# Hash attention and routed experts on one core: order of the small transfers at the start, queue of one small input, cut of the output stores

## The chip, the core and the metric

The kernel runs on one core of a Trainium2 chip. The metric is the device time of one execution in microseconds (us), and lower is better. The kernel before took 804.9 us (median of three runs, 802.9 to 805.1). Engines are named as the profile names them: PE is TensorE (matmuls), DVE is VectorE, ACT is ScalarE, POOL is GpSimd, SP is the sync engine. SPq, ACTq and POOLq are their queues of DMA issues. The core's 16 DMA engines serve all of these queues.

A profile is one execution under the hardware profiler. Its times count from the start of the span, and its span is about 1.7 us shorter than the timed execution (804.0 against 805.68 us for the kernel before).

## The reference, cut to what matters

```python
# q, k, v: (4, 8, 768, 64) float32; proj: (64, 6)
q_bits = (einsum('bhsd,dk->bhsk', q, proj) > 0)      # six hash bits for each row
k_bits = (einsum('bhsd,dk->bhsk', k, proj) > 0)
mask = bucket(q_bits)[..., :, None] == bucket(k_bits)[..., None, :]
attn = softmax(where(mask, q @ k.T / 8, -1e9));  x = attn @ v        # -> (3072, 512)
P = sinkhorn(exp(x @ w_gate - max))                  # eight rounds, 8 experts
out = sum over e of P[:, e] * (relu(x @ w1[e]) @ w2[e])              # (3072, 512)
```

## The kernel before

Attention goes first, in eight head groups of four heads each. The PE work of a group is 24 units of scores, exp and values. For a group's scores the kernel needs q and k transposed with the head dimension on partitions, and their hash bits beneath them in the same tile. DVE transposes 32x32 blocks, POOL casts to float16, and small DMAs ("stackings", 48 KB each) move the blocks of each head to partitions 0 to 63. The bits are computed by float32 matmuls with `pb`, which is built from `proj`, written to DRAM in one transfer ("put") and read back per head ("bit transfers"). This is the head of the kernel and one group's preparation:

```python
for c in range(2):
    pin(nc.sync.dma_start(out=proj4[:, c, :], in_=proj[32*c:32*(c+1), :].unsqueeze(0)
                          .to_broadcast([HG, 32, NB])))          # HG = 4
nc.vector.memset(pb, 0.0)
for a in range(HG):                                              # DVE copies of proj
    nc.vector.tensor_copy(pb[32*a:32*(a+1), :, a, 0:NB], proj4[32*a:32*(a+1)])
# ...
def stack(name, c):
    for h in range(HG):
        pin(eng(name).dma_start(out=d[name][32*c:32*(c+1), h, :],
                                in_=t16s[name][32*h:32*(h+1), c, :]))
def get_bits(name):
    for h in range(HG):
        pin(eng(name).dma_start(out=d[name][D:KR, h, :]..., in_=dss[name][:, h, 0:NB+1, :]...))
# ... prepare(n), in pieces between the units of group n - 1 (group 0: all at once)
turn_qk("k", 0);  stack("k", 0);  turn_qk("k", 1)
if n: stack("k", 1);  fetch(n + 1, "k")                          # fetch: POOL's queue
turn_qk("q", 0);  turn_qk("q", 1)
hashed("k");  put_bits("k")
if n == 0: stack("k", 1);  get_bits("k")
stack("q", 0);  hashed("q");  put_bits("q");  stack("q", 1)
if n: fetch(n + 1, "q");  get_bits("k")
get_bits("q");  cast_v();  fetch(n + 1, "v" if n else "kqv")
```

`pin` keeps the order of the program on each queue.

The experts come after that. In the last expert each block of 128 output rows is stored as it is ready. Row r*24 + j*4 + m of a batch lies on partition m*32 + r, so the output side of a store has the dimensions (m: 4, r: 32, columns: 512):

```python
outv = out.rearrange("(b r j m) d -> b j m r d", b=B, r=R, j=J)
# in the fused blocks (batches 0 to 2 of the last expert), two stores of 256 KB each:
pin(nc.sync.dma_start(out=outv[b, j], in_=sums_of(b, j).rearrange("p c d -> p (c d)")))
# in final() (the last batch), six blocks, the last in two halves of the columns:
pin((nc.sync if cols.start == 0 else nc.scalar).dma_start(out=outv[b, j][:, :, cols], in_=dst[:, cols]))
```

The softmax here doesn't subtract the row's maximum and nothing guards it: scores larger than these inputs give would overflow.

Of the kernel before, what the change touches and what calls it, by code (L numbers as in the profile page):

```python
# [20 lines left out]
def kernel(  # L21
# [11 lines left out]
    nc = tc.nc  # L33
    B, H, S, D = q.shape
    assert (B, H, S, D) == (4, 8, 768, 64)
    NB = proj.shape[1]
# [4 lines left out]
    DD = H * D  # L41
# [9 lines left out]
    HG = 4  # L51
    NGRP = H // HG
    R = 32
    M = S // R
    KT = S // P
    M4 = P // R
    QT = S // HG
    KR = D + NB + 1
# [4 lines left out]
    def pin(ins):  # L63
        tc.keep_in_program_order(ins)
        return ins
# [2 lines left out]
    pb = consts.tile([P, 2, HG, 8], F32)  # L68
    proj4 = consts.tile([P, 2, NB], F32)
    for c in range(2):  # L70
        pin(nc.sync.dma_start(out=proj4[:, c, :], in_=proj[32 * c:32 * (c + 1), :].unsqueeze(0)
                              .to_broadcast([HG, 32, NB])))
    nc.vector.memset(pb, 0.0)
    for a in range(HG):
# [50 lines left out]
    outv = out.rearrange("(b r j m) d -> b j m r d", b=B, r=R, j=J)  # L125

    def sums_of(b, j):
        if j < J // 2:
            return acc[:, b, j, 0:2, :]
        return acc[:, b, j - J // 2, 2:4, :]  # L130

    def quarters_of_w(e):

# [94 lines left out]
    def mixed(e, b):  # L228

        wq = weights[e, "t"]  # L230
        pw = pw_[-1]
        for i in range(J // 2):
            hq = hsums[e, b, i]
            plo, phi = pw[:, b * J + i, e:e + 1], pw[:, b * J + J // 2 + i, e:e + 1]
            if e == 1:
                for j in (i, J // 2 + i):
                    pin(nc.scalar.activation(out=sums_of(b, j), in_=sums_of(b, j), func=Act.Copy,
                                             scale=pw[:, b * J + j, 0:1]))
            a = yps.tile([P, DD // 2], F32, tag="y", name="a")
            d1 = yps.tile([P, DD // 2], F32, tag="y", name="d1")  # L240
            y2 = y2ps.tile([P, DD // 2], F32, tag="y", name="y2")
            vt = vkeep.tile([P, 4, DD // 2], F32, tag="v", name="vt")

            def prod(dst, hn, wn, first):
                for fo in range(FH):
                    pin(nc.tensor.matmul(dst, hq[hn][:, fo, :], wq[wn][:, fo, :], start=first and fo == 0,  # L246
                                         stop=fo == FH - 1, skip_group_check=True))

            def keep(k, p):
                pin(nc.scalar.activation(out=vt[:, k], in_=a, func=Act.Copy, scale=p))  # L250

            def gather(k, src, p):
                dst = acc[:, b, i, k, :]
                pin(nc.vector.scalar_tensor_tensor(out=dst, in0=src, scalar=p, in1=dst, op0=Alu.mult, op1=Alu.add))  # L254

            def step(name):
                if name == "a1":
                    prod(a, "h11", "b11", True)
                    keep(0, plo)
                elif name == "a2":  # L260
                    prod(a, "s2", "t2", False)
                    keep(2, phi)
                elif name == "a3":
                    prod(a, "s1", "t1", False)
                    keep(3, phi)
                elif name == "a4":
                    prod(a, "s4", "b22", False)
                    keep(1, plo)
                elif name == "d":
                    prod(d1, "h12", "b21", True)  # L270
                    gather(0, d1, plo)
                elif name == "y":
                    prod(y2, "s3", "t3", True)
                    gather(3, y2, phi)
                else:
                    prod(y2, "h22", "t4", False)
                    gather(2, y2, phi)

            for g, name in enumerate(ORDERS[i]):
                step(name)  # L280
                if g == 4 and i + 1 < J // 2:
                    sums_of_h(e, b, i + 1)
                if g == 6:
                    if e < E - 1:
                        pin(nc.gpsimd.dma_start(out=acc[:, b, i], in_=vt, accum_op=Alu.add))  # L285
                    else:
                        eng = nc.vector if i == J // 2 - 1 else nc.gpsimd
                        pin(eng.tensor_tensor(acc[:, b, i], acc[:, b, i], vt, op=Alu.add))
                        for j in (i, J // 2 + i):
                            pin(nc.sync.dma_start(out=outv[b, j],  # L290
                                                  in_=sums_of(b, j).rearrange("p c d -> p (c d)")))
                    next(coming)
                yield 433

    def final():

        e, b = E - 1, B - 1
        w2, hT = weights[e, 2], hts[e, b]
        for j in range(J):
            yp = (yps if j % 3 < 2 else y2ps).tile([P, DD], F32, tag="y", name="yp")  # L300
            dst = sums_of(b, j).rearrange("p c d -> p (c d)")
            for cols in ((slice(0, DD),) if j < J - 1 else (slice(0, DD // 2), slice(DD // 2, DD))):
                for fo in range(FO):
                    pin(nc.tensor.matmul(yp[:, cols], hT[:, fo, j * P:(j + 1) * P], w2[:, fo, cols],
                                         start=(fo == 0), stop=(fo == FO - 1), skip_group_check=True))
                pin(nc.vector.scalar_tensor_tensor(out=dst[:, cols], in0=yp[:, cols],
                                                   scalar=pw_[-1][:, b * J + j, e:e + 1], in1=dst[:, cols],
                                                   op0=Alu.mult, op1=Alu.add))
                pin((nc.sync if cols.start == 0 else nc.scalar).dma_start(out=outv[b, j][:, :, cols],
                                                                          in_=dst[:, cols]))  # L310
            yield

    def first_hidden(b):
# [49 lines left out]
    def prepare(n):  # L363

        d = grp[n] = {}
        va, vs = vas[n % 2], vss[n % 2]
        trs, bts, dss, t16s = {}, {}, {}, {}
# [2 lines left out]
            d[name] = wk.tile([P, HG, S], F16, tag=name + "s", name=name + "s")  # L370
            t16s[name] = wk.tile([P, 2, S], F16, tag="t16", name="t16")

        def eng(name):
            return nc.scalar if n == 0 and name == "q" else nc.sync

        def turn_qk(name, c):
            i_ap = nat[name, n][:, :, 32 * c:32 * (c + 1)]
            o_ap = trs[name][:, c, :]
            if name == "k":
                i_ap = i_ap.rearrange("p (m t) d -> p m t d", m=M4)  # L380
                o_ap = o_ap.rearrange("p (t m r) -> p m t r", t=KT, m=M4)
            else:
                o_ap = o_ap.rearrange("p (m r) -> p m r", r=R)
            pin(nc.vector.transpose(o_ap, i_ap))  # L384
            pin(nc.gpsimd.tensor_copy(t16s[name][:, c, :], trs[name][:, c, :]))  # L385

        def stack(name, c):
            for h in range(HG):
                pin(eng(name).dma_start(out=d[name][32 * c:32 * (c + 1), h, :],  # L389
                                        in_=t16s[name][32 * h:32 * (h + 1), c, :]))  # L390

        def hashed(name):
            pr = ops.tile([P, 512], F32, tag="o", name="pr")
# [14 lines left out]
            pin(eng(name).dma_start(out=ds.rearrange("j h r t -> (j h r) t"), in_=bts[name]))  # L408
            dss[name] = ds

        def get_bits(name):
            for h in range(HG):
                pin(eng(name).dma_start(out=d[name][D:KR, h, :].rearrange("r (j t) -> r j t", j=HG),
                                        in_=dss[name][:, h, 0:NB + 1, :].rearrange("j r t -> r j t")))

        def cast_v():
            v32 = wk.tile([P, HG, 3, D], F32, tag="v32", bufs=1)
# [10 lines left out]
        lag = 2 if n > 2 else 1  # L428
        yield 0
        turn_qk("k", 0)  # L430
        stack("k", 0)
        yield lag
        turn_qk("k", 1)
        if n:
            stack("k", 1)
            if n + 1 < len(groups):
                fetch(n + 1, "k")
        yield 2 * lag
        turn_qk("q", 0)
        yield 3 * lag  # L440
        turn_qk("q", 1)
        yield 2 + 3 * lag
        hashed("k")
        put_bits("k")
        if n == 0:
            stack("k", 1)
            get_bits("k")
        stack("q", 0)
        yield 4 + 3 * lag
        hashed("q")  # L450
        put_bits("q")
        stack("q", 1)
        if n and n + 1 < len(groups):
            fetch(n + 1, "q")
        yield 6 + 3 * lag
        if n:
            get_bits("k")
        get_bits("q")
        cast_v()
        if n + 1 < len(groups):  # L460
            fetch(n + 1, "v" if n else "kqv")
# [92 lines left out]
    for _ in prepare(0):  # L554
        pass
    warm = ops.tile([P, 512], F32, tag="o", name="warm")
    for _ in range(12):
        pin(nc.tensor.matmul(warm, ident, vas[1].rearrange("p h t d -> p (h t d)")[:, 0:512],
                             start=True, stop=True))

# [9 lines left out]
    for u in range(len(units) + 1):  # L570
        if u < len(units):
            n, h, kt = units[u]
            b, g = groups[n]
# [24 lines left out]
        elif u >= 2 * per:  # L598
            owed += (total if b < 3 else total - 12 * 865) / (2 * per - 8)
            while owed > 0:  # L600
                c = next(fill, None)
# [199 lines left out]
```

## Time and profile before

| what | before | view |
|---|---|---|
| span | 804.0 us | page |
| first score matmul | 21.07 us | timeline |
| first scores of group 1 | 48.24 us, after 6.07 us of idle PE | timeline |
| first scores of group 2 | 70.3 us | timeline |
| last DVE instruction ends | 787.7 us | timeline |

The page of the kernel before: span, PE's busy time, its busy tenths in 40 slices of 20 us, the granted clock in tenths, and the busy share of the DMA engines in tenths.

```profile
span 804.0 us, 16754 instructions
...
PE   3969999999999999999999999999999999999991
...
PEclk9779999999989999999999999999999999999996
DMA  6966676641002264486468657745964676541222
```

PE is busy 90% of the time or more except in the first and third slice and in the last one. The change aims at the time there. The timeline of the kernel before at the start (start, duration, engine, line, operation, output<-input, and in brackets the engine's idle time ahead of it and what ended it):

```profile
0.80 1.38 SPq L71 DMA_DIRECT2D proj<-in_proj_dram  x2
2.22 0.48 SPq L354 DMA_DIRECT2D acc<-in_k_dram  x1
...
4.05 0.98 DVE L76 COPY pb<-proj 32x12 f32<-32x12 f32 x4 [3.05 <-DMA proj<-in_proj_dram]
...
6.60 1.84 DVE L384 STREAM_TRANSPOSE acc<-acc 128x768 f32<-128x768 f32 x2 [0.82 <-DMA acc<-in_k_dram]
...
10.02 3.69 SPq L389 DMA_DIRECT2D ks<-t  x4
...
21.07 1.44 PE L473 MATMUL st<-qs,ks 71*128 71x384 f16 x4 [4.84 <-DMA qs<-ds]
...
48.24 0.80 PE L473 MATMUL st<-qs,ks 71*128 71x384 f16 x2 [6.07 <-DMA qs<-ds]
```

`proj` is 6 KB with its four copies, goes first in the sync queue and is there at 4.05 us. Both starts of scores wait for bits of q (`qs<-ds`). The windows view of the kernel before (stretch, length, then busy time and instructions of PE, PEld, DVE, ACT and POOL; then the granted clock, the busy share of the DMA engines, and GB/s):

```profile
50.00:52.00 2.00, 2.00 (x18) 1.22 (x16) 1.26 (x3) 1.41 (x2) 0.00 (x0) 0.50 0.00 0
5.00:8.00 3.00, 0.36 (x8) 0.20 (x8) 2.05 (x7) 0.00 (x0) 0.35 (x1) 1.00 0.99 400
788.00:790.00 2.00, 0.00 (x0) 0.00 (x0) 0.00 (x0) 0.00 (x0) 0.00 (x0) 0.99 0.26 102
```

The first line shows a clock of 0.50 after the idle gap. In the third, only stores run, on a quarter of the DMA engines' time at a quarter of the rate of the second. The timeline of the kernel before at its end, DVE's last instruction and the last store issues:

```profile
778.67 14.92 SPq L309 DMA_DIRECT2D out_dram<-acc  x6
...
787.24 0.48 DVE L306 SCALAR_TENSOR_TENSOR acc<-yp,p,acc 128x256 f32<-128x256 f32 x1 [1.13 <-PE yp L304]
```

Six issues take 14.92 us, and the span ends 16.3 us after the last computation.

### The profile page before, as it was taken

The page shows a single profiled execution, that of the slowest core. Times are in us where ns is not written, and L with a number is a line of the kernel's source. Part 1 is how long each engine was busy: PE and PEld are TensorE (multiplying, and loading weights), DVE is VectorE, ACT ScalarE, POOL GpSimd, SP SyncE. Part 2 cuts the span into 40 slices and gives each one's busy share as a digit, 9 for nine tenths or more (in the row PEclk, how much of TensorE's full clock was granted, in tenths as well). Part 3 has the DMA queues.
Part 4 walks back from the last instruction along what each step waited for, and adds up shares of the span by engine and source line. Part 5 has one row for each costly group of instructions (what it writes and reads, how often), then busy time and mean ns, then how long its engine had stood idle before and what let it go on. Part 6 is the DMA issues. An engine that isn't in the chain of part 4 may idle for free.

```text
span 804.0 us, 16754 instructions
## 1 busy us (share of the span) xinstructions
PE 756.1 (94%) x6384; PEld 523.1 (65%) x6384; DVE 531.0 (66%) x1198; ACT 509.1 (63%) x1022; POOL 310.1 (39%) x314
## 2 busy tenths in 40 slices
PE   3969999999999999999999999999999999999991
PEld 1546656656655677777777777777777777777750
DVE  3334555645458677777777777777777777778760
ACT  0758666767844677766666666666666666666530
POOL 7645356238300133344444334344434434242220
PEclk9779999999989999999999999999999999999996
DMA  6966676641002264486468657745964676541222
GB/s 169 268 161 150 145 196 159 140 113 51 2 2 52 42 111 84 81 156 106 93 112 139 115 96 133 122 94 96 162 106 83 121 139 106 95 89 62 84 80 92
DMA packets 42636, 88.56 MB, mean 110 GB/s; under 512 B 9852, under 2 KB 22908, under 8 KB 42556
## 3 DMA queue, kind: packets, MB, share of 16 engines
q0 software_dynamic: 27440, 71.06, 45.6%
q1 hardware_dynamic: 14316, 15.82, 7.0%
q8 instruction: 50, 0.82, 0.4%
q10 hardware_dynamic: 800, 0.62, 0.3%
q14 instruction: 30, 0.25, 0.1%
HBM read 53.14 MB, written 7.08 MB: 75 GB/s over the span
## 4 chain that ended last, share of the span: by engine, by line
PE 79%; DMA 6%; ACT 5%; DVE 2%; POOL 2%; SPq 2%; issue 2%; POOLq 0%; ACTq 0%; DVEq 0%
PE a L679 18%; PE a L246 17%; PE d L679 13%; PE y L246 8%; PE st L473 5%; PE d L246 4%; PE hp L531 4%; PE yp L206 3%; ACT pt L476 2%; PE num L489 2%; DMA qs<-t 2%; PE hp L321 2%; DMA qs<-ds 1%; PE yp L541 1%; SPq L389 1%
## 5 line engine op out<-in xcount | busy, mean ns | idle before, releaser
L688 DVE CUSTOM_DVE_ANT_0 hT<-d,u 128x384 f16<-128x384 f32 x336 | 185.6, 553 | 99.8 <-ACT u L684 98.1
L250 ACT ACTIVATE vt<-a,p 128x256 f32<-128x256 f32 x324 | 153.3, 473 | 149.2 <-PE a L246 148.9
L476 ACT ACTIVATE pt<-st 128x768 f16<-128x768 f32 x192 | 147.1, 809 | 71.7 <-PE st L473 51.3
L684 ACT COPY u<-a 128x384 f32<-128x384 f32 x336 | 160.9, 479 | 22.4 <-PE a L679 20.1
L285 POOL DMA_DIRECT2D acc<-vt x72 | 61.4, 852 | 267.9 <-ACT vt L250 112.3
L246 PEld LDWEIGHTS <-hT 128*128 128x128 f16 x1296 | 126.3, 97 | 50.7 <-DVE hT L688 1.1
L246 PE MATMUL a<-t,hs 128*128 128x256 f16 x972 | 145.8, 272 | 2.0 <-ACT vt L250 1.5
L246 PEld LDWEIGHTS <-hs 128*128 128x128 f16 x972 | 94.8, 98 | 38.3 <-issue 2.8
L473 PE MATMUL st<-qs,ks 71*128 71x384 f16 x384 | 98.0, 338 | 15.9 <-DMA qs<-ds 11.7
L679 PEld LDWEIGHTS <-t 128*128 128x128 f16 x896 | 87.7, 98 | 36.1
L679 PE MATMUL a<-xT,s 128*128 128x384 f16 x448 | 109.4, 326 | 0.1
L679 PE MATMUL d<-xd,t 128*128 128x384 f16 x448 | 109.4, 326 | 0.0
L246 PE MATMUL y<-t,hT 128*128 128x256 f16 x648 | 97.1, 272 | 0.0
L254 DVE SCALAR_TENSOR_TENSOR acc<-y,p,acc 128x256 f32<-128x256 f32 x162 | 77.4, 478 | 11.4 <-PE y L246 11.4
L489 PEld LDWEIGHTS <-pt 128*128 128x128 f16 x1152 | 62.5, 99 | 28.4 <-issue 3.7
L679 PEld LDWEIGHTS <-s 128*128 128x128 f16 x672 | 65.5, 97 | 17.6 <-issue 2.3
L489 PE MATMUL num<-va,pt 128*128 128x65 f16 x1152 | 68.4, 196 | 0.6 <-ACT pt L476 0.6
L385 POOL CAST t<-acc 128x768 f16<-128x768 f32 x32 | 26.3, 826 | 89.5 <-DVE acc L384 89.3
L473 PEld LDWEIGHTS <-ks 71*128 71x128 f16 x384 | 33.4, 100 | 37.1 <-issue 14.7
L718 ACT ACTIVATE hT<-a 128x384 f16<-128x384 f32 x112 | 54.0, 482 | 1.8 <-PE a L679 1.7
L679 PE MATMUL a<-xd,s 128*128 128x384 f16 x224 | 54.3, 323 | 0.7 <-ACT u L684 0.5
L679 PE MATMUL a<-xT,t 128*128 128x384 f16 x224 | 54.7, 326 | 0.0
(97 smaller groups left out, 981.2 us busy)
## 6 DMA issues: line engine op xcount, KB each, us to landing
acc<-vt POOLq DMA_DIRECT2D x72, 512.0 KB, 4.6
t<-in_moe_w_dram POOLq DMA_DIRECT2D x24, 512.0 KB, 7.5
out_dram<-acc SPq DMA_DIRECT2D x23, 256.0 KB
acc<-in_k_dram POOLq DMA_DIRECT2D x7, 768.0 KB, 5.6
acc<-in_q_dram POOLq DMA_DIRECT2D x7, 768.0 KB, 6.0
v<-in_v_dram POOLq DMA_DIRECT2D x28, 192.0 KB, 4.6
t<-in_moe_w_dram POOLq DMA_DIRECT2D x4, 1024.0 KB, 10.1
ks<-t SPq DMA_DIRECT2D x64, 48.0 KB
```

The source lines that it names most:

```text
L246: pin(nc.tensor.matmul(dst, hq[hn][:, fo, :], wq[wn][:, fo, :], start=first and fo == 0, stop=fo == FH - 1, skip_group_check=True))
L250: pin(nc.scalar.activation(out=vt[:, k], in_=a, func=Act.Copy, scale=p))
L254: pin(nc.vector.scalar_tensor_tensor(out=dst, in0=src, scalar=p, in1=dst, op0=Alu.mult, op1=Alu.add))
L285: pin(nc.gpsimd.dma_start(out=acc[:, b, i], in_=vt, accum_op=Alu.add))
L473: pin(nc.tensor.matmul(st[:, i, 0:HT], d["k"][0:KR, h, kt * P:(kt + 1) * P], d["q"][0:KR, h, i * HT:(i + 1) * HT], start=True, stop=True))
L476: pin(nc.scalar.activation(out=pt, in_=st[:, :, 0:HT], func=Act.Exp, scale=scale))
L489: pin(nc.tensor.matmul(num[:, j * (D + 1):(j + 1) * (D + 1)], pf[:, j * P:(j + 1) * P], va[:, h, kt, :], start=(kt == 0 and j == 0), stop= ...
L531: pin(nc.tensor.matmul(hp[:, 0:HT], w1[:, do, fo * P:(fo + 1) * P], xT[:, do, b * S + t * HT:b * S + (t + 1) * HT], start=(do == 0), stop= ...
L679: pin(nc.tensor.matmul(bk, wq[wn][:, do, f * P:(f + 1) * P], xq[xn][:, do, :], start=first and do == 0, stop=do == 1, skip_group_check=True))
L684: pin(nc.scalar.copy(t, bk))
L688: pin(add(TENSOR_ADD_SAT, out=dst, in0=bk, in1=u, s0=3e38, s1=0.0))
L718: pin(nc.scalar.activation(out=hT[:, f, hi], in_=a, func=Act.Relu))
```

## The change

It has three parts. Head-by-head order: each operand's first head is stacked and gets its bits first, so that scores can begin before the other heads are ready; in group 0, q's first two heads go on ACT's queue and the rest on SP's. `proj` moves to ACT's queue, so that the first large load is issued earlier. A store is cut into four transfers of 32 partitions.

```diff
-        pin(nc.sync.dma_start(out=proj4[:, c, :], in_=proj[32 * c:32 * (c + 1), :].unsqueeze(0)
+        pin(nc.scalar.dma_start(out=proj4[:, c, :], in_=proj[32 * c:32 * (c + 1), :].unsqueeze(0)
...
+    def put_rows(b, j, src, cols, engs):
+        for m in range(M4):
+            pin(engs[m % len(engs)].dma_start(out=outv[b, j][m][:, cols], in_=src[R * m:R * (m + 1), cols]))
...   (fused blocks: put_rows(..., (nc.sync,));  final(): put_rows(..., (nc.sync, nc.scalar)))
-            return nc.scalar if n == 0 and name == "q" else nc.sync
+            return nc.scalar if n == 0 and name == "q" and h < 2 else nc.sync
...
-        def stack(name, c):
-            for h in range(HG):
+        def stack(name, h):
+            for c in range(2):
...   (get_bits(name, h): one head, no loop)
         turn_qk("k", 1)
+        stack("k", 0)
         if n:
             stack("k", 1)
...
         turn_qk("q", 1)
+        stack("q", 0)
...      (both puts, stack("k", 1) for n == 0, stack("q", 1), stack("k", 2), fetch of q)
+        get_bits("k", 0);  get_bits("q", 0);  get_bits("k", 1);  get_bits("q", 1)
+        stack("k", 3);  stack("q", 2);  get_bits("k", 2);  get_bits("q", 2)
+        stack("q", 3);  get_bits("k", 3);  get_bits("q", 3)
         cast_v()
...
-    for _ in range(12):          # warm-up matmuls
+    for _ in range(14):
```

More of the change, by code (lines that the diff above doesn't have):

```diff
@@ L289, in mixed @@
                         for j in (i, J // 2 + i):
-                            pin(nc.sync.dma_start(out=outv[b, j],
-                                                  in_=sums_of(b, j).rearrange("p c d -> p (c d)")))
+                            put_rows(b, j, sums_of(b, j).rearrange("p c d -> p (c d)"), slice(0, DD), (nc.sync,))
                     next(coming)
@@ L308, in final @@
                                                    op0=Alu.mult, op1=Alu.add))
-                pin((nc.sync if cols.start == 0 else nc.scalar).dma_start(out=outv[b, j][:, :, cols],
-                                                                          in_=dst[:, cols]))
+                put_rows(b, j, dst, cols, (nc.sync, nc.scalar))
             yield
@@ L371, in prepare, with eng @@
             t16s[name] = wk.tile([P, 2, S], F16, tag="t16", name="t16")
-        def eng(name):
-            return nc.scalar if n == 0 and name == "q" else nc.sync
+        def eng(name, h=0):
+            return nc.scalar if n == 0 and name == "q" and h < 2 else nc.sync
         def turn_qk(name, c):
@@ L385, in turn_qk @@
             pin(nc.gpsimd.tensor_copy(t16s[name][:, c, :], trs[name][:, c, :]))
-        def stack(name, c):
-            for h in range(HG):
-                pin(eng(name).dma_start(out=d[name][32 * c:32 * (c + 1), h, :],
-                                        in_=t16s[name][32 * h:32 * (h + 1), c, :]))
+        def stack(name, h):
+            for c in range(2):
+                pin(eng(name, h).dma_start(out=d[name][32 * c:32 * (c + 1), h, :],
+                                           in_=t16s[name][32 * h:32 * (h + 1), c, :]))
         def hashed(name):
@@ L409, in put_bits, with get_bits @@
             dss[name] = ds
-        def get_bits(name):
-            for h in range(HG):
-                pin(eng(name).dma_start(out=d[name][D:KR, h, :].rearrange("r (j t) -> r j t", j=HG),
-                                        in_=dss[name][:, h, 0:NB + 1, :].rearrange("j r t -> r j t")))
+        def get_bits(name, h):
+            pin(eng(name, h).dma_start(out=d[name][D:KR, h, :].rearrange("r (j t) -> r j t", j=HG),
+                                       in_=dss[name][:, h, 0:NB + 1, :].rearrange("j r t -> r j t")))
         def cast_v():
@@ L430, in prepare @@
         turn_qk("k", 0)
-        stack("k", 0)
         yield lag
         turn_qk("k", 1)
+        stack("k", 0)
         if n:
@@ L446, in prepare @@
             stack("k", 1)
-            get_bits("k")
-        stack("q", 0)
         yield 4 + 3 * lag
@@ L452, in prepare @@
         stack("q", 1)
+        stack("k", 2)
         if n and n + 1 < len(groups):
@@ L455, in prepare @@
         yield 6 + 3 * lag
-        if n:
-            get_bits("k")
-        get_bits("q")
+        get_bits("k", 0)
+        get_bits("q", 0)
+        get_bits("k", 1)
+        get_bits("q", 1)
+        stack("k", 3)
+        stack("q", 2)
+        get_bits("k", 2)
+        get_bits("q", 2)
+        stack("q", 3)
+        get_bits("k", 3)
+        get_bits("q", 3)
         cast_v()
```

## The prediction

> **What bounds it now.** TensorE is busy 94% of the span (page, part 1), from 73 to 785 us practically always (windows). The change touches the two ends, where it idles.
>
> *Start.* The timeline shows the first score matmul at 21.07 us, 4.84 us after the warm-up matmuls, released by q's bit transfer. At the second head group TensorE idles again from 42.17 to 48.24 us (waits view: q's bits). After both gaps the windows view shows a granted clock of 0.50 for 7.5 to 8 us; a unit (scores, exp, values) then takes 0.97 us instead of about 0.74. The Trainium skill, "TensorE: Matmul & The Clock Gate", Part 1, says that an idle array is throttled; this trace agrees (1.00 to 0.50 near 18.6 and 45.9 us).
>
> *End.* The last VectorE instruction ends at 787.72 us, the span at 804.0. In those 16.3 us only stores run. From 772 us the windows view shows a DMA share of 0.26 and 102 GB/s, against 0.99 and 400 GB/s at 5 to 8 us: 4 of 16 engines. The Trainium skill, "DMA: Bandwidth & Descriptors", "Why a DMA increments its semaphore by 16 and not by 1", says that the number of engines must divide the slowest dimension of both sides; the store's output side starts with a dimension of 4. The trace agrees. Ten stores of 256 KB at 102 GB/s are 25.7 us: a backlog.
>
> **What changes.**
> 1. proj on ScalarE's queue: the first input load is issued at 0.80 instead of 2.22 us; k, q and v land 1.42 us earlier.
> 2. First head first: before group 0's scores, 13 sync transfers (0.5 to 0.6 us each to issue) and 10 on ScalarE had queued; k's first stacking waited until 10.02 us behind a v load (4.5 us). Now head 0 needs about 8 and 6. First score estimated at 16 us, right behind the 14 warm-ups, clock still 1.00.
> 3. Group 1: GpSimd fetches its inputs after v's cast, so only 1.4 us earlier. TensorE will wait about 3 us at group 1's hash matmuls (k transposed near 23.6 us), a new stall. But q's first bits come after 14 sync issues instead of 24: landing near 39 us instead of 48.16, as TensorE arrives (39.5 to 41). The 6.07 us stall and the second cold stretch (about 2 us) go. Group 2 starts near 61 instead of 70.3 us: **gain 9.3 us**, kept, since TensorE is then the bound.
> 4. Stores of 32 partitions: 16 engines, bandwidth no longer matters; the issues do: four of about 0.6 us per 256 KB. The last two fused blocks put 16 on the sync queue (772.8 to 782.5), then 14 follow: last issue near 791 on the old time axis, end by 794. Tail 6.3 us instead of 16.3: **gain 9.8 us**.
>
> **Sum.** 804.9 - 9.3 - 9.8 = 785.8 us; range 780 to 791. Faster by over 2% (under 788.8): 0.8; within 2%: 0.19; slower: 0.01.
>
> **What would show it.** First score at 15 to 17.5 us; idle before group 1's scores under 2 us; clock 1.00 there; TensorE waiting for transposes near 21 to 24 us; group 2 starting 8 to 11 us earlier; last VectorE instruction to end of span 5 to 7.5 us.
>
> **What would make it wrong.** Bit transfers still delayed by the input fetches and the weight load (DMA share about 1.0 from 21 to 46 us), so that group 1 still stalls; the new stall dropping the clock; store issues dearer than 0.6 us, or ScalarE's waiting for the sync queue's; issues of 0.35 us would shorten the tail further.

## The result

The changed kernel took 792.86 us (median of four runs, 792.05 to 795.91), against 804.5 us before (four runs). The ratio is 0.9865, with a 95% interval from 0.9835 to 0.9895. A ratio in this document is the mean time of one kernel's fast runs over that of the other's in the same rounds, so it is not quite the ratio of the medians. The gain is real but below 2%, and the time lies above the predicted range of 780 to 791.

The changed kernel's page, its timeline at the start, its windows view, and DVE's last instruction in its timeline:

```profile
span 791.1 us, 16872 instructions
...
PE   1789999999989999999999999999999999999996
...
PEclk9999999999999999999999999999999999999999
DMA  4896766651003164496458646764775496443335
```

```profile
0.81 0.41 SPq L356 DMA_DIRECT2D acc<-in_k_dram  x1
0.81 1.82 ACTq L71 DMA_DIRECT2D proj<-in_proj_dram  x2
...
14.62 0.70 DVE L76 COPY pb<-proj 32x12 f32<-32x12 f32 x4 [13.62 <-DMA proj<-in_proj_dram]
...
15.99 3.55 DVE L386 STREAM_TRANSPOSE acc<-acc 128x768 f32<-128x768 f32 x4
...
25.70 0.81 PE L482 MATMUL st<-qs,ks 71*128 71x384 f16 x4 [0.84 <-DMA ks<-ds]
...
49.89 0.48 PE L482 MATMUL st<-qs,ks 71*128 71x384 f16 x2 [1.48 <-DMA qs<-ds]
```

```profile
11.00:14.00 3.00, 0.00 (x0) 0.00 (x0) 0.00 (x0) 0.00 (x0) 0.00 (x0) 1.00 0.14 36
50.00:54.00 4.00, 4.00 (x35) 2.60 (x34) 1.99 (x4) 2.68 (x4) 0.40 (x1) 0.57 1.13 223
776.00:780.00 4.00, 4.00 (x21) 1.80 (x19) 2.05 (x3) 0.00 (x0) 0.00 (x0) 1.00 0.71 194
```

```profile
785.23 0.48 DVE L309 SCALAR_TENSOR_TENSOR acc<-yp,p,acc 128x256 f32<-128x256 f32 x1 [1.12 <-PE yp L307]
```

The end became as short as was hoped: the span ends 5.4 us after the last DVE instruction instead of 16.3, which is 10.9 us. From 776 to 780 us the stores move 194 GB/s at a DMA share of 0.71, where the windows view of the kernel before has 99 GB/s at 0.28 in the same stretch. The start didn't. k's load is issued 1.4 us earlier, but DVE's copies of `proj` wait until 14.62 us instead of 4.05, and the transposes of k and q stand behind them. The DMA share of 0.14 from 11 to 14 us shows that most of the DMA engines' time is free by then, while `proj` and a remainder of the loads still trickle in, and the four transposes run without any wait once the copies are done. PE's first score comes 4.6 us later than before. The idle time ahead of group 1 shrinks from 6.07 to 1.48 us, so that group 2 starts at 69.7 us, 0.6 us earlier, and all computation ends 2.0 us earlier (785.7 against 787.7). 10.9 + 2.0 is the 12.9 us between the two spans.

### The profile page after: what moved, and what is told of

The parts are those of the page before. It is cut to its first block, busy times and chain, and to the rows that moved or that the text cites. A ratio compares the mean times of both kernels' runs of the same rounds, so it can differ in the third digit from the quotient of the medians.

```text
span 791.1 us, 16872 instructions
## 1 busy us (share of the span) xinstructions
PE 752.1 (95%) x6386; PEld 520.8 (66%) x6386; DVE 529.0 (67%) x1198; ACT 509.1 (64%) x1022; POOL 310.3 (39%) x314
## 4 chain that ended last, share of the span: by engine, by line
PE 84%; ACT 7%; DMA 4%; DVE 2%; issue 1%; POOL 1%; SPq 0%; ACTq 0%; DVEq 0%; POOLq 0%
PE a L688 18%; PE a L250 17%; PE d L688 13%; PE y L250 9%; PE st L482 6%; PE d L250 4%; PE hp L540 4%; ACT pt L485 4%; PE num L498 3%; PE yp L550 3%; PE yp L210 3%; PE hp L323 2%; DMA proj<-in_proj_dram 2%; ACT acc L241 1%; PE pr L398 1%
## 5 line engine op out<-in xcount | busy, mean ns | idle before, releaser
L482 PE MATMUL st<-qs,ks 71*128 71x384 f16 x384 | 95.3, 330 | 7.2 <-ACT pt L485 3.5
L688 PE MATMUL d<-xT,t 128*128 128x384 f16 x224 | 54.7, 326 | 0.0
```

What stands on the lines that cost most here:

```text
L482: pin(nc.tensor.matmul(st[:, i, 0:HT], d["k"][0:KR, h, kt * P:(kt + 1) * P], d["q"][0:KR, h, i * HT:(i + 1) * HT], start=True, stop=True))
L688: pin(nc.tensor.matmul(bk, wq[wn][:, do, f * P:(f + 1) * P], xq[xn][:, do, :], start=first and do == 0, stop=do == 1, skip_group_check=True))
```

## The experiments

Milestones of all kernels below, in us, read from the timelines (first score matmul of groups 0, 1 and 2; end of the last DVE instruction; span). Each row is one profile. The kernel before and c_stores have the same program up to the stores and differ by up to 1.3 us; d_heads' profile is the slowest of its four runs (800.8 us, the median is 796.63):

| kernel | group 0 | group 1 | group 2 | last DVE | span |
|---|---|---|---|---|---|
| before | 21.1 | 48.2 | 70.3 | 787.7 | 804.0 |
| changed | 25.7 | 49.9 | 69.7 | 785.7 | 791.1 |
| c_stores | 20.6 | 49.5 | 71.5 | 786.4 | 791.7 |
| d_heads | 18.8 | 44.2 | 65.9 | 782.8 | 799.1 |
| b_proj_act | 31.2 | 56.1 | 78.0 | 798.4 | 813.6 |
| a2_proj_sync | 17.5 | 42.7 | 64.5 | 780.4 | 785.8 |
| f_proj_wait | 20.8 | 46.9 | 68.0 | 785.0 | 790.4 |
| g_proj1 | 15.3 | 41.6 | 64.6 | 780.3 | 785.8 |
| e_proj8 | 18.7 | 43.4 | 64.8 | 781.7 | 787.3 |
| h_fetch_early | 23.8 | 44.8 | 64.3 | 780.3 | 785.8 |
| l_w_late | 15.4 | 40.5 | 60.4 | 778.6 | 784.2 |
| r_fetch2_late | 15.4 | 39.1 | 58.3 | 777.4 | 782.8 |
| m_tail | 15.5 | 41.1 | 62.8 | 779.9 | 783.3 |

### One part at a time

The theory is that `proj` is late because it shares its DMA engines with the input loads, and that this costs what the start should have gained. The rival is that the head-by-head order gains little in any case. Four kernels were run on one chip, with three rounds each.

The changed kernel with one line undone:

```diff
-        pin(nc.scalar.dma_start(out=proj4[:, c, :], ...
+        pin(nc.sync.dma_start(out=proj4[:, c, :], ...
```

> The changed kernel with one line undone: proj is fetched on the sync queue again, ahead of k, q and v. Theory 1 (proj on ScalarE's queue shares its four DMA engines with the 2.3 MB of input loads, lands only when they are through, at 14.5 us, and holds back everything behind VectorE's copies of it): proj lands near 4 us as before, the first score falls from 25.7 to 17 to 18 us, group 1 starts near 42 to 44 instead of 49.9 us, and the total is about 785 us (784 to 787). Theory 2 (the head-by-head order itself gives little, because the bit transfers and the cast of the next group wait for transfers under the fetches in any case): the first score comes earlier, but group 1's scores still start near 48 us and the total stays within 791 to 793 us.

Measured: 788.55, 789.42 and 790.12 us in the timed rounds. The profiled run (876.2 us, clock 0.846) isn't used. That is outside what either theory had expected, between the two. It was therefore run again:

> The first run of this kernel (changed kernel, proj on the sync queue) had a slow profile and timed runs of 788.6 to 790.1 us; theory 1 had expected 784 to 787. Again, for a fast profile and beside the runs below: 788 to 790 us; first score near 18.5 us, group 2 near 64 to 66 us, against 25.7 and 69.7 in the changed kernel.

Measured: 787.54 us (787.32 to 790.03), slightly below the expected 788 to 790, ratio to before 0.978 (0.9754 to 0.9807). From its timeline:

```profile
4.04 1.00 DVE L76 COPY pb<-proj 32x12 f32<-32x12 f32 x4 [3.04 <-DMA proj<-in_proj_dram]
...
17.50 0.81 PE L482 MATMUL st<-qs,ks 71*128 71x384 f16 x4 [1.31 <-DMA ks<-ds]
```

`proj` is there at 4.04 us, the first score comes at 17.5 us, 8.2 us earlier than in the changed kernel, and group 2 at 64.5 us, 5.2 us earlier. Of the 8.2 us, 3 are lost on the way; the part on groups 1 and 2 below deals with that.

The kernel before with only `proj` moved:

```diff
-        pin(nc.sync.dma_start(out=proj4[:, c, :], ...
+        pin(nc.scalar.dma_start(out=proj4[:, c, :], ...
```

> The kernel before with only proj moved to ScalarE's queue. Theory 1: proj lands near 14 us, the first score moves from 21.07 to about 30 us, and the total rises by 6 to 9 us to about 811 to 813. Theory 2 (proj's place does not matter, since the start was bound by other waits): 803 to 806 us.

Measured: 814.61 us against 803.72 us for the kernel before (ratio 1.0106, 1.0067 to 1.0146): theory 1, and somewhat more than its 811 to 813 us. From the timeline of this run, the copies of `proj` and the first score:

```profile
14.64 0.70 DVE L76 COPY pb<-proj 32x12 f32<-32x12 f32 x4 [13.63 <-DMA proj<-in_proj_dram]
```

```profile
31.25 1.44 PE L473 MATMUL st<-qs,ks 71*128 71x384 f16 x4 [7.11 <-DMA qs<-ds]
```

Moving 6 KB to another queue makes the kernel slower by 8.5 us (by the ratio) to 10.9 us (by the medians): the first score comes 10.2 us later and the last DVE instruction 10.7 us.

The kernel before with only the stores cut (the `put_rows` lines of the diff):

> The kernel before with only the stores cut to 32 partitions. If the stores' gain is the whole of the gain at the end: the stretch from the last VectorE instruction to the end of the span falls from 16.3 to 5.4 us, the total to 793.5 us (792.5 to 794.5), everything before the stores unchanged (first score at 21.07 us, last VectorE instruction at 787.7 us). A rival (cutting a store in four only costs issues, and the four engines are not the limit): over 800 us.

Measured: 792.8 us, ratio 0.9857 (0.9826 to 0.9888). The last DVE instruction ends at 786.4 us, the span at 791.7: 5.3 us. From its page and timeline:

```profile
span 791.7 us, 16836 instructions
...
785.91 0.48 DVE L309 SCALAR_TENSOR_TENSOR acc<-yp,p,acc 128x256 f32<-128x256 f32 x1 [1.13 <-PE yp L307]
```

This part alone accounts for the gain at the end, as expected.

The kernel before with only the order changed (the rest of the diff, without `proj` and stores):

> The kernel before with only the order of stackings and bit transfers changed (and 14 warm-up matmuls). Theory 1: first score at 17 to 18 us, last VectorE instruction 8 us earlier (near 780), total about 796.5 us (795 to 798). Theory 2: last VectorE instruction at 786 to 788 us, total within 2 us of the kernel before.

Measured: 796.63 us, with a wide spread (794.17 to 800.8), ratio 0.9904 (0.9862 to 0.9946). The first score comes at 18.8 us and the last DVE instruction ends at 782.8 us, 4.9 us earlier than before; 8 had been expected. But this profile is of the slowest of the four runs. The median of 796.63 us is what theory 1 had expected (795 to 798), 7.1 us below the kernel before (7.7 by the ratio). The rival falls.

The medians differ from the 803.72 us of the kernel before in the same rounds by -10.9 (stores), -7.1 (order) and +10.9 us (`proj`). These add up to -7.1, while the whole change gave -11.6. Stores and order simply add: -18.0 as a sum, and -18.2 in a2_proj_sync, which has both (787.54 against 805.72). Only the price of `proj` differs: 10.9 us with the old order, and with the new one 5.3 us (792.86 - 787.54; 4.6 to 6.8 by the ratios 0.9808 and 0.978 of the two runs with `proj` on the sync queue against 0.9865). That the rest disappears in waits that would have come anyway is likely, but not shown.

### Why proj is late

The Trainium skill, "DMA: Bandwidth & Descriptors", section "Queues, rings and completion order", says that a DMA engine takes turns between the queues that have work for it, packet by packet. The section "Rules for kernel authors" says that an outermost dimension of c < 16, "e.g. a leading zero-stride broadcast of c copies", confines a DMA to at most c engines. `proj` is such a broadcast of four. By this reading its 256 packets of 24 bytes stand in four engines, 64 in each, and each waits for a turn behind packets of the input loads. The records of packets do not name the engine, so the 64 in each are an estimate from that rule and not shown. On the sync queue they were ahead of the loads in one queue. The trace's packet records, counted by size, show when the 24-byte packets moved (this is a count over the records, not a view of the profile):

```
kernel         packets of 24 bytes   first moved   last moved    median time of one
before                256               2.27 us       3.60 us          9 ns
changed               256               4.68 us      13.72 us          9 ns
f_proj_wait           256               2.29 us       3.93 us          9 ns
e_proj8               256               2.38 us       7.02 us          9 ns
g_proj1                64               2.59 us       3.93 us          9 ns
```

The packets are not slower in the changed kernel (9 ns each at the median), they come up more rarely: 256 in 9.0 us instead of 1.3. The same records show the turns: from 11 to 14 us the changed kernel moves 69 packets of 24 bytes and 70 of 1536 bytes (the loads of v), and in order of time they alternate nearly one by one. The first packet too is late, 4.68 us against 2.59 in g_proj1, with the issue at 0.81 and 0.80 us; why was not looked into. And the loads suffer as well: of the 256 packets of 6144 bytes that bring k and q, half were through at 4.8 us instead of 6.1, but the last at 11.2 us instead of 8.1. All this leaves a rival: ACT's queue itself might be slow, with its table load right behind. Two runs separate the two. A third was to separate the number of engines from the number of packets.

The first holds back the loads. The edit:

```diff
+    hold = scr.tile([P, 2, NB], F32, tag="hold", name="hold")
+    pin(nc.sync.dma_start(out=hold, in_=proj4))
     fetch(0, "kqv", nc.sync)
```

> The changed kernel, proj still on ScalarE's queue, but sync's first input load is held until proj has landed (a small transfer out of proj's tile goes ahead of it in the same queue). If proj is late because it shares its DMA engines with the input loads: with them held, proj lands by 4 us and VectorE's copies of it start at about 4 us. If ScalarE's queue itself is late (its activation table load, or a first transfer that starts slowly there): the copies start at 12 us or later still. Total in the first case near 790 to 792 us, since the inputs come 1.5 to 2.5 us later than in the kernel before; in the second near 805.

Measured: one run, 792.11 us. From its timeline:

```profile
0.81 1.79 ACTq L71 DMA_DIRECT2D proj<-in_proj_dram  x2
4.33 0.35 SPq L563 DMA_DIRECT2D hold<-proj  x1
4.38 0.70 DVE L76 COPY pb<-proj 32x12 f32<-32x12 f32 x4 [3.38 <-DMA proj<-in_proj_dram]
```

The same two transfers on the same queue, and `proj` is there at 4.38 us. ACT's queue isn't slow; the loads are what delays it. This shows the cause and is no cure: k's load is now issued at 4.73 us, and the total is about that of the changed kernel.

The second makes it small and wide:

```diff
-    for c in range(2):
-        pin(nc.scalar.dma_start(out=proj4[:, c, :], in_=proj[32 * c:32 * (c + 1), :].unsqueeze(0)
-                              .to_broadcast([HG, 32, NB])))
+    pin(nc.scalar.dma_start(out=proj4[0:32], in_=proj.rearrange("(c p) n -> p c n", c=2)))
...
-        nc.vector.tensor_copy(pb[sl, :, a, 0:NB], proj4[sl])
+        nc.vector.tensor_copy(pb[sl, :, a, 0:NB], proj4[0:32])
```

> The changed kernel, proj on ScalarE's queue as one transfer of 32 partitions (64 packets of 24 bytes over 16 engines, where the changed kernel has 256 over 4), and VectorE's four copies spread it. The input loads are not held. If the number of packets in each engine's queue decides how late proj is (64 in each of four engines took until 14.5 us): 4 packets in each of 16 engines land before 5 us, k's transposes start near 5.8 us, the first score comes near 17.5 us, the total is 0 to 2 us below that of proj on the sync queue, 787 to 789.5 us. If any transfer beside the input loads waits until they are through: copies near 12 us, total about 792.

Measured: 787.31 us (784.39 to 787.6), ratio 0.9759 (0.9726 to 0.9791). From its timeline:

```profile
0.80 0.43 ACTq L70 DMA_DIRECT2D proj<-in_proj_dram  x1
0.81 0.40 SPq L354 DMA_DIRECT2D acc<-in_k_dram  x1
...
4.56 0.70 DVE L74 COPY pb<-proj 32x12 f32<-32x12 f32 x4 [3.56 <-DMA proj<-in_proj_dram]
```

Here `proj` and k are issued at the same time and `proj` still lands early. So it is not any transfer beside the loads that is late; but this edit makes the packets fewer (64) and their engines more at once. The first score comes at 15.34 us, the earliest of these kernels. The prediction had 16.

The third keeps the 256 packets but cuts them into eight transfers of 32 partitions, so that they can spread over 16 engines:

```diff
+    for a in range(HG):
+        for c in range(2):
+            pin(nc.scalar.dma_start(out=proj4[32 * a:32 * (a + 1), c, :], in_=proj[32 * c:32 * (c + 1), :]))
```

> The changed kernel, proj on ScalarE's queue in eight transfers of 32 partitions (256 packets, 16 in each of 16 engines). By the number of packets in a queue: between the two, the copies start at 5 to 8 us. If the number of engines does not matter, only the number of packets in all: 14 us as in the changed kernel.

Measured: one run, 788.99 us. The four copies start between 6.33 and 8.51 us, slightly beyond the expected 5 to 8 at the end. That lies between the other two, as the number of packets in one engine's queue by the skill's rule would have it (64, 16 and 4: last packet at 13.72, 7.02 and 3.93 us). But this run does not decide it: its eight issues took until 5.4 us, and its v loads were issued at 6.22 us instead of 1.73. By the packet records 135 of its 256 packets moved from 6.5 to 7.0 us, when the loads of k and q were through and those of v had hardly begun. Whether `proj` is late for the number of its packets or for the few engines that they stand in stays open.

### Which dimension sets the stores' rate

```diff
-        for m in range(M4):
-            ... out=outv[b, j][m][:, cols], in_=src[R * m:R * (m + 1), cols]
+        for m in range(2):
+            ... out=outv[b, j][2 * m:2 * m + 2][:, :, cols], in_=src[2 * R * m:2 * R * (m + 1), cols]
```

> The kernel before with its stores cut in two of 64 partitions, whose output side starts with a dimension of 2. If that dimension sets the number of DMA engines: 2 of 16, a DMA share of 0.13 and about 51 GB/s in the stores' stretches, and so a backlog that grows through the last expert: the end of the span comes 60 us or more after the last VectorE instruction, total over 845 us. If smaller transfers or two queues are what helped: 793 to 804 us.

Measured: one run, 855.51 us. The last DVE instruction ends at 784.8 us, the span 69.0 us later. A line of its windows view, long after the computation:

```profile
800.00:820.00 20.00, 0.00 (x0) 0.00 (x0) 0.00 (x0) 0.00 (x0) 0.00 (x0) 0.50 0.13 51
```

Share 0.13 and 51 GB/s are half of the 0.26 and 102 of the kernel before: two engines, four engines. A cut in two makes matters worse; what helps is that the outer dimension of each transfer is 32. The rule in the skill's section "Why a DMA increments its semaphore by 16 and not by 1" holds in both cases.

### What still holds back groups 1 and 2

With `proj` early (g_proj1), group 0 starts 2.2 us earlier than with `proj` on the sync queue (a2), but group 2 starts at the same time. PE arrives at group 1 about 2 us before its bits. The first trial fetched group 1's inputs earlier:

```diff
+        if n == 0:
+            fetch(1, "kq")
         cast_v()
         if n + 1 < len(groups):
-            fetch(n + 1, "v" if n else "kqv")
+            fetch(n + 1, "v")
```

> The kernel with proj in one small transfer, and group 1's k and q are fetched before v's cast on GpSimd (v after it, as before). What holds group 1 at 41.6 us though the first score comes at 15.3 us? Theory A (the time at which its inputs are fetched, 16.4 us): the fetch starts near 9.6 us, TensorE's wait at the hash matmuls (7 and 2.3 us in all 9.2 with the first one) falls to under 1 us past the first, group 1 starts near 37 to 39 us and the total falls by 2 to 4 us to 783.5 to 785.5. Theory B (the transfers of stackings and bits are slow beside any fetch): the first score moves to 18 to 20 us, group 1 starts at 41 us or later, and the total stays at 786.5 to 789 us.

Measured: 787.51 us, no gain over g_proj1 (787.31; its repeat, i_tail below, took 787.34). From its waits view:

```profile
PE st L482 <- DMA qs<-ds: 10.0, 1, 10.0
```

The fetch starts at 10.3 us, and now group 0's bits travel beside it: PE waits 10.0 us for them, and the first score moves to 23.8 us, further than theory B had said. Group 0 and group 1 together take 40.5 us from there instead of 49.3, but that only makes up for the late start. The second and third trials take traffic away from group 1's bits instead. In `l_w_late` the weight load of group 1's preparation is issued one group later; in `r_fetch2_late` group 2's k and q also follow group 1's bit transfers:

```diff
-        if n in (1, 3):
-            load_w(0, (n + 1) // 2, pin=True)
+        if n in (2, 3):                        # l_w_late and r_fetch2_late
+            load_w(0, n - 1, pin=True)
...     # r_fetch2_late alone: fetch(n + 1, "k") and fetch(n + 1, "q") at their old places only for n > 1
-            fetch(n + 1, "v" if n else "kqv")
+            fetch(n + 1, "v" if n > 1 else "kqv")
```

> The kernel with proj in one small transfer; the 2 MB load of the first expert's weights is issued one group later (it was issued at 36.3 us, beside the bit transfer of q that took 5.1 us to land and released group 1's scores at 41.6). If that load slows the bit transfer: it lands in 2.5 to 3.5 us, group 1 starts near 39.5 us; gain up to 2 us. If the input fetches of group 2 alone do it: group 1 starts at 41 to 42 us again, 787 us.

> As l_w_late, and group 2's k and q are fetched after group 1's bit transfers are out (they were issued at 24.1 and 27.8 us, before them). Theory B (stackings and bits are slow because the fetches fill the DMA engines, share about 1.0): the put of k's bits lands in about 2 to 3 us instead of 6.75, q's first bits come near 35 us, and group 1 starts at 37.5 to 39.5 us instead of 41.6. Rival (the chain is a matter of issues and waits in the sync queue): group 1 starts at 41 us or later. Whether the total falls is open: group 2's inputs come later; 783.5 to 788 us.

Measured: 785.13 us (783.1 to 785.88) and 786.44 us (784.55 to 789.83). The windows view over the time in which group 1's bits travel, first in g_proj1, then in r_fetch2_late:

```profile
28.00:36.00 8.00, 7.38 (x99) 5.08 (x96) 1.73 (x4) 7.39 (x11) 7.16 (x13) 1.00 0.91 259
```

```profile
28.00:36.00 8.00, 7.32 (x99) 5.03 (x96) 1.40 (x4) 7.91 (x11) 7.37 (x13) 1.00 0.34 82
```

And the chain that ended last, in g_proj1, from the put of k's bits to the landing of q's:

```profile
29.12 6.75 DMA ds<-kb
...
36.33 5.14 DMA qs<-ds
```

With the share at 0.91 a put takes 6.75 us and a read of 10 KB 5.14. At 0.34, the first read is issued 4.4 us after the put (27.64 to 32.03 us in the timeline of r_fetch2_late; 6.8 us in g_proj1; theory B had said a put of 2 to 3 us):

```profile
27.64 1.18 SPq L408 DMA_DIRECT2D ds<-kb  x1
...
32.03 0.43 SPq L412 DMA_DIRECT2D ks<-ds  x1
...
39.13 0.48 PE L480 MATMUL st<-qs,ks 71*128 71x384 f16 x2
```

Group 1 starts at 39.1 us without any wait for bits, and the clock stays at 1.00 from 36 to 48 us: group 2 starts at 58.3 us instead of 64.6. So traffic is what slows the bits, as theory B said; without it the bits came less early than expected. In l_w_late group 1 started at 40.5 us, between the two expectations, and group 2 at 60.4. The total doesn't follow: the waits view of r_fetch2_late shows PE waiting 2.8 us for the gate's weights (`wg_sb`), which come later now, and group 3 starts at 89.1 us against 90.8. Most of the 6.3 us are given back there. Where the rest of them goes, beyond those 2.8 us, was not looked into.

### What is left at the end

> The kernel with proj in one small transfer, and the last fused block's stores shared between the sync and ScalarE's queues (ScalarE has no more work by then). In the changed kernel the sync queue issued until 788.7 us, 3 us after VectorE's last instruction, and the span ended 5.4 us after it. If those issues are what is left at the end: that stretch falls to 3.5 to 4.2 us and the total by 1.2 to 2 us, to about 785.5. If the landing of the last store is: unchanged within 0.5 us.

> The two edits together: their gains should add, since they lie at opposite ends: 782 to 784.5 us by theory A with the issues, 785 to 787 by theory B with the issues.

These two edits were to share the last fused block's stores between two queues, but they named the last batch, whose stores are made elsewhere. They changed nothing, and the runs are repeats of g_proj1 and h_fetch_early: 787.34 and 786.66 us. Group 2 started at 63.0 us in the repeat of g_proj1, whose own profile has 64.6: two profiles of one program differ by 1.6 us at that point. The edit with the right batch:

```diff
-  put_rows(b, j, ..., slice(0, DD), (nc.sync,))
+  put_rows(b, j, ..., slice(0, DD), (nc.sync, nc.scalar) if b == B - 2 and i == J // 2 - 1 else (nc.sync,))
```

> What the run i_tail was to be: that edit named the last batch, whose stores don't come from the fused blocks, and so changed nothing. Now the last fused block's stores (last batch but one) are shared between the sync and ScalarE's queues. If the sync queue's backlog of issues is what is left at the end: from VectorE's last instruction to the span's end 3.5 to 4.2 us instead of 5.5; total down by 1.2 to 2 us. If the landing of the last store is: unchanged within 0.5 us.

Measured: 784.72 us (783.34 to 786.4), ratio 0.9752 (0.9728 to 0.9776). From its timeline:

```profile
777.69 2.99 SPq L132 DMA_DIRECT2D out_dram<-acc  x6
777.70 3.06 ACTq L132 DMA_DIRECT2D out_dram<-acc  x6
...
779.40 0.48 DVE L308 SCALAR_TENSOR_TENSOR acc<-yp,p,acc 128x256 f32<-128x256 f32 x1 [1.12 <-PE yp L306]
```

Both queues end their issues together at 780.7 us, and the span ends 3.4 us after DVE's last instruction instead of 5.5. The backlog of issues on the sync queue was what remained. The total can't be told apart from that of g_proj1 (0.9759); the 2.1 us are read from the profile.

> r_fetch2_late and m_tail together. If both gains hold and group 2 is not held back: 782 to 785 us; if group 2 waits for its late inputs, what the start gains is lost there, and 785 to 787 us remain.

Measured: 784.98 us (783.49 to 786.24), ratio 0.9759 (0.9734 to 0.9785): no better than m_tail. Its profile has the shortest span, 781.8 us, but the timed runs don't confirm a difference. m_tail (small wide `proj`, shared last stores, all else as in the change) is a version that beats both kernels clearly and simply: 0.9752 of the kernel before, where the changed kernel is 0.9865, and their intervals don't touch.

## Why the prediction was wrong, point by point

- **Step 1 failed.** It said "proj on ScalarE's queue: the first input load is issued at 0.80 instead of 2.22 us; k, q and v land 1.42 us earlier". The issue is so (0.81 us), but the last packet of k and q was through at 11.2 us instead of 8.1. And what was missing is a term for `proj` itself: it was taken to land as before, and it landed 10.6 us later (copies at 14.62 instead of 4.05 us). The prediction had no wait of `proj` behind the loads that now ran beside it. It did name the rule that a leading dimension of four confines a transfer to four engines, applied it to the stores, and didn't ask what it meant for the broadcast of four. f_proj_wait shows that the loads beside it are the cause, and g_proj1 that a smaller and wider transfer escapes them; b_proj_act gives the price on the old order (8.5 to 10.9 us), and a2_proj_sync on the new one (5.3 us, both between the medians, 792.86 - 787.54, and between the spans, 791.1 - 785.8).
- **Step 2's first score** was 25.7 us instead of 16. Its arithmetic was about right once `proj` is out of the way: 15.3 us in g_proj1, with `proj` early and the loads early as step 1 had them.
- **Step 3's gain of 9.3 us** was 2.0 us. With `proj` on the sync queue it is 7.3 us (787.7 - 780.4). The remaining 2 us are not traced to one cause. Its sizes for transfers under load were too small: group 1's start came at 42.7 us instead of 39.5 to 41, with put and read of the bits at 6.75 and 5.14 us while fetches fill the DMA engines (both in g_proj1). But in r_fetch2_late, where that start was mended, the total hardly moved. The new stall at the hash matmuls that it expected is there (1.90 us in the changed kernel), and the clock is at 0.50 from 34 to 36 us, which the prediction had named among the things that would make it wrong.
- **The second cold stretch** was to go. It didn't in the changed kernel: the windows line of 50 to 54 us shows a clock of 0.57. The waits view has one gap of 1.48 us right before it.
- **Step 4 was right**, and a little better than predicted: 5.4 us of tail instead of 6.3, a gain of 10.9 instead of 9.8. An issue took 0.42 us at the median, not 0.6. What bounds the tail is the sync queue's issues, as it said; m_tail shows it.
- **The sum.** 9.3 + 9.8 were predicted, 2.0 + 10.9 measured. With step 1's fault undone (a2_proj_sync), the time is 787.5 us, inside the predicted range and 1.7 us above its centre.

## What to carry to other kernels

Before a small transfer is moved to another queue, ask what stood behind it and what will now run beside it: ahead of the loads in one queue, `proj` was there at 4.05 us; in a second queue, where it shared DMA engines with them packet by packet, at 14.62. Look at the outermost dimension on both sides of every transfer, of a broadcast too: here it set the rate of the stores (a dimension of 4: 102 GB/s; of 2: 51 GB/s), and by the skill's rule it also decides in how many engines a small transfer waits beside large ones (here 9 us for 256 packets, their number and their engines not told apart). And where an engine works in order, as DVE does here, the smallest input can hold back the largest: read from the timeline what the first instruction waits for, not only which load is the biggest.

## What the Trainium skill lacked or had wrong

- "DMA: Bandwidth & Descriptors", section "Queues, rings and completion order", gives the turns by packet but no price. Here the two kinds of packets alternate nearly one by one late in the loads, and 256 packets of 24 bytes in a second queue took 9.0 us beside the input loads (4.68 to 13.72 us) and 1.3 us ahead of them (2.27 to 3.60 us); if they stand 64 to an engine, as that page's rule says, that is an estimated 0.14 us of waiting for each.
- The same page, "Issuing engines are not separate DMA queues", says that initiating on several engines "will only save the time on the sequencer". In b_proj_act a move of 6 KB to a second queue cost 8.5 to 10.9 us: the order of one queue was worth more than the issue time saved (1.4 us). The section doesn't warn of this.
- The same page, "Rules for kernel authors", advises against cutting a transfer by partitions ("Don't bother") and for one of 128 partitions. That presumes that 16 engines are in use, which the same table's line on the outermost dimension (quoted above) asks for, without linking the two. Where the other side's outer dimension was 4, four transfers of 64 KB took 10.9 us off the kernel (c_stores), and two of 128 KB added some 50 (j_stores64, 855.5 us).
- No page gives the landing time of small transfers while large ones fill the engines. Here, at a DMA share of 0.91, a 48 KB put to DRAM took 6.75 us and a 10 KB read 5.14 us.
- "TensorE: Matmul & The Clock Gate", Part 1, puts the lowering of the clock after an idle window of about 3.4 us. In the changed kernel the clock was lower already after a shorter gap: the waits view shows 1.48 us of it before group 1's scores (49.89 us), and the mean clock from 50 to 54 us is 0.57; in the kernel before, the clock fell 2.3 us after the last warm-up matmul (16.2 to 18.6 us).
